# Full-height edge products with zero padding in a fused attention and MLP kernel

## The chip, the cores and the metric

One core of one Trainium2 chip runs the program. The metric is the device time of one execution in microseconds (us); the kernel before was timed three times.

## The reference

Eight batches, eight heads of 64 elements, 512 local and 32 global tokens per batch. A local query sees the local keys within 32 places of it and all 32 global keys; a global query sees every key. Each has its own softmax. The attention output of all 4352 tokens then goes through an MLP with a GELU and weights of 512 x 2048 and 2048 x 512.

```python
k_all = np.concatenate([k_g, k_l], axis=2)
out_g = np.matmul(sm(scale * np.matmul(q_g, k_all.transpose(0, 1, 3, 2))), np.concatenate([v_g, v_l], axis=2))
s_ll = np.where(np.abs(pos[:, None] - pos[None, :]) <= 32, scale * np.matmul(q_l, k_l.transpose(0, 1, 3, 2)), -1e9)
a_l = sm(np.concatenate([scale * np.matmul(q_l, k_g.transpose(0, 1, 3, 2)), s_ll], axis=-1))
out_l = np.matmul(a_l, np.concatenate([v_g, v_l], axis=2))
x = np.concatenate([out_g, out_l], axis=2).transpose(0, 2, 1, 3).reshape(B * S, H * D)
return gelu(x @ w_in) @ w_out
```

## The kernel before

**Numbers.** All products run in float32r. An operand is split into a rounded part (hi) and the rest (lo), and two or three partial products are summed.

**Units and chunks.** The attention of the local queries goes in 64 units, each of one batch, one half (256) of its 512 local queries and one pair of heads. The MLP goes in 17 chunks of 256 tokens, 16 of them a half batch each, the last the global queries of all batches. While TensorE works on the MLP of one half batch, the units of the next are made beside it. The MLP's products are `ml_h` (L865 to L867, three products of 256 columns for each of 4 row blocks) and `ml_o` (L889 to L891, 512 columns); its intermediate goes through ScalarE's GELU (`gf`), a rounding copy (`gh`, L379 to L381) and GpSimd's subtraction (`gl`, L386).

**A unit** loads its keys and queries, transposes them, and makes scores (`st_s`, L605: twelve products of 64 rows, the two heads of the pair on rows 0 to 63 and 64 to 127). Mask, exponential and scaling follow. `st_t` (L688 to L691) transposes the weights on TensorE, `st_ah` and `st_al` (L702) copy and split them into `at`, and `st_o` (L719) multiplies them with the values `vs`. `st_c` and `st_x` bring the output `o` into `xs`, which the MLP reads.

**The edge product of a unit.** A unit has two tiles of 128 queries. One tile sits next to an end of the sequence and sees 64 keys besides its own 128 (32 global ones, 32 neighbours): `st_o` of each head has three products over 128 rows and a fourth over these 64 edge keys. The values of the 64 edge keys lie in one slot of `vs`, head 0 in partitions 0 to 63 and head 1 in 64 to 127; the matching weights lie the same way in `at0[:, :, 3]`. The fourth product so reads 64 rows, `er = slice(64 * j, 64 * j + 64)` (L713, L717).

**Values.** `load_v` (L505) brings a unit's values into `vr` (7 slots of 64 elements), `split_v` (L527) makes `vs`: a copy for the hi part (L529; by ScalarE for the units of the first batch, by VectorE later) and a subtraction on GpSimd for the lo part (L530). The buffers of `vr`, two of them, are shared with the values of the global queries and with the output tile `ob`.

**Global queries.** `gu_o` (L823) makes five products for a pair of heads: four over 128 keys, the fifth over the 32 that remain, `a[:k, n]` with k = 32.

**Order.** Every step has a place in a list (`at`, L921), set by a table of offsets; the list sets the order of TensorE's instructions exactly (L1059), and of the table functions on ScalarE. The order of the other instructions on VectorE, ScalarE, GpSimd and the DMA queue of SyncE is worked out by a scheduler that takes each when it finds it ready.

Of the kernel before, what the change touches and what calls it, by code (L numbers as in the profile page):

```python
# [8 lines left out]
F32 = mybir.dt.float32  # L9
F32R = mybir.dt.float32r  # L10
# [7 lines left out]
# Products run in float32r. An operand x is split exactly into hi = round(x)  # L18
# and lo = x - hi, which float32r both holds without loss, and the partial
# products of the parts are summed in float32.  # L20
#
# Attention goes by units (batch, half of its local queries, pair of heads),
# the MLP by chunks of 256 tokens (a half batch; the global queries of all
# batches make the last chunk).  Units of one half batch are worked out while
# the MLP of the half batch before is on the tensor engine.
#
# A unit has two tiles of 128 queries: "simple" (next to an end of the
# sequence) and "full".  Blocks of 32 keys, G = the global keys:
#   half 0: keys [0 1 2 3 G 4 5 6 7 8]
#       simple window [0 1 2 3 G 4]        edge rows (G, 4)  # L30
#       full window   [3 G 4 5 6 7 8]      edge rows (3, G, 8, -)
#   half 1: keys [7 8 9 10 11 G 12 13 14 15]
#       simple window [11 G 12 13 14 15]   edge rows (11, G)
#       full window   [7 8 9 10 11 G 12]   edge rows (-, 7, G, 12)
NB = 10            # key blocks of a unit
WS, WF = 192, 224  # window widths
# [3 lines left out]
# Places of the steps in the order of the program, relative to their plain  # L40
# places, and (E_) the engines of steps that several engines can do.
# [282 lines left out]
def attn_mlp(ctx, tc, q_l, k_l, v_l, q_g, k_g, v_g, w_in, w_out, out):  # L324
    nc = tc.nc
# [4 lines left out]
    P = 128  # L330
# [23 lines left out]
    for half in range(2):  # L354
        m = cp.tile([P, WS + WF], BF16, name=f"mask{half}")
        nc.gpsimd.memset(m, 0.0)
        # (column, first key block's distance in keys from the tile's first
        # query, width) of the local key runs of the windows
        if half == 0:
            runs = [(0, 0, 128), (160, 128, 32),  # L360
                    (WS, -32, 32), (WS + 64, 0, 160)]
        else:
            runs = [(0, -32, 32), (64, 0, 128),
                    (WS, -32, 160), (WS + 192, 128, 32)]
        for c0, k0, w in runs:
            v = m[:, c0:c0 + w]
            # keep where q - k + 32 >= 0 and k - q + 32 >= 0
            nc.gpsimd.affine_select(out=v, in_=v, pattern=[[-1, w]], base=32 - k0,
                                    channel_multiplier=1, compare_op=ALU.is_ge, fill=-BIG)
            nc.gpsimd.affine_select(out=v, in_=v, pattern=[[1, w]], base=32 + k0,  # L370
                                    channel_multiplier=-1, compare_op=ALU.is_ge, fill=-BIG)
        masks.append(m)
# [30 lines left out]
    # They come as float64; word 1 of an element has sign, exponent and the  # L403
    # first 20 bits of the fraction.  As a float32 pattern times 2^-112 its
    # exponent has float32's offset, and three bits further to the left it is
    # the float32 pattern, lacking three bits of word 0 and the sign.
    # Blocks of 512 elements are kept as hi | lo.
# [49 lines left out]
    vs = cp.tile([P, 7, 2, D], F32R, name="vs")  # L457
# [4 lines left out]
    sgr = [cp.tile([P, R], F32, name=f"sgr{j}") for j in range(2)]  # L462
    gs = cp.tile([P, NP, P], F32R, name="gs")
# [3 lines left out]
    def late_tiles():  # L467
        # in the place of the weights' raw words
        wx.close()
        lp = ctx.enter_context(tc.tile_pool(name="lp", bufs=1))  # L470
        late["xg"] = lp.tile([P, NP, CH], F32, name="xg")
        late["vgs"] = lp.tile([P, 10, 2, D], F32R, name="vgs")
        late["agt"] = lp.tile([P, 5, 2, 2, SG], F32R, name="agt")

    # Blocks of 32 tokens x 32 elements of a pair of heads, for the transposes
    # of blocks: partitions are (head, half of the elements, token).
# [25 lines left out]
    # Values: slots are (tile 0, head 0), (tile 0, head 1), (tile 1, ...), the  # L502
    # full tile's edge rows for head 0 and 1, the simple tile's edge rows with
    # head 0 in the lower and head 1 in the upper partitions.
    def load_v(u):  # L505
        b, half, p = u
        raw = ap_.tile([P, 7, D], F32, name="vr", tag="vr", bufs=2)
# [15 lines left out]
        for r0, src, s0 in es:  # L523
            for j in range(2):
                nc.sync.dma_start(out=raw[64 * j + r0:64 * j + r0 + 32, 6, :], in_=src[j, s0:s0 + 32, :])
# [6 lines left out]
    def st_v(u):  # L532
        split_v((u,), vs, 7)

    # Exponentials and gelus stay in the order in which they are written here:
    # each change between them is a load of ScalarE's tables.
# [38 lines left out]
    def st_tg(b):  # L575
        # columns of a pair's scores for the globals: (hi, lo), head, query
# [8 lines left out]
    def windows(half):  # L585
        # (first key column, width, query tile) of the simple and the full tile
        if half == 0:
            return (0, WS, 0), (96, WF, 1)
        return (128, WS, 1), (0, WF, 0)

    # both heads at once (j = 0): the heads of a pair are on different rows of the tensor engine
# [17 lines left out]
    # columns of the simple and the full tile's windows; 224:256 stays zero  # L609
# [5 lines left out]
    def own(half):  # L615
        # columns of the tiles' own keys
        return (256, 64) if half == 0 else (96, 288)
# [87 lines left out]
    def st_o(u, j):  # L705
# [7 lines left out]
        er = slice(64 * j, 64 * j + 64)  # L713
# [3 lines left out]
              (vs[er, 6], at0[er, :, 3, :], qs)]  # L717
# [4 lines left out]
    # o holds [V hi; V lo] x [A hi | A lo]  # L722
# [60 lines left out]
    def gu_t(g, i):  # L783
        # transposes of one pair's rows: [key, (head, query)]
# [31 lines left out]
    # o: rows (head, A hi or lo, query), columns (head, V hi or lo, element)  # L816
    def gu_o(g, i):
        a = late["agt"]
        o = ps_s.tile([P, 2, 2, D], F32, name="go", tag="s")
        st[g, "o"] = o  # L820
        for n in range(5):
            k = P if n < 4 else 32
            nc.tensor.matmul(out=o, lhsT=a[:k, n].rearrange("p h l q -> p (h l q)"),  # L823
                             rhs=late["vgs"][:k, 2 * n:2 * n + 2], start=(n == 0), stop=(n == 4))
# [116 lines left out]
    for n, u in enumerate(units):  # L941
# [3 lines left out]
        # places between the MLP's products  # L945
# [148 lines left out]
```

## Time and profile before

| | |
|---|---|
| time, median of 3 runs | 1170.29 us (1169.29 to 1170.46) |
| span of the profiled execution | 1168.5 us, first to last instruction; no separate time of that execution is on record |
| PE (TensorE) busy | 1072.6 us, 92% |
| DVE (VectorE), ACT (ScalarE), POOL (GpSimd) busy | 775.4, 648.8, 444.2 us |
| granted TensorE clock, mean | 0.992 |

The rows of the profile name an engine, a line of the kernel, the operation, what is written and read (`o<-at,vs`), its rows and columns in the array (`64*128`), and the size of what streams through. PEld is the load of a product's stationary operand, which runs beside the products. A row of the timeline begins with the start in us from the span's start and the duration; equal neighbours are merged, with their count behind an x. Products overlap in it: each is drawn with a latency of some 0.28 us while the next starts 0.12 us after it, so distances between starts, not durations, tell what a product costs the engine.

### The profile page before, as it was taken

The page shows a single profiled execution, that of the slowest core. Times are in us where ns is not written, and L with a number is a line of the kernel's source. Part 1 is how long each engine was busy: PE and PEld are TensorE (multiplying, and loading weights), DVE is VectorE, ACT ScalarE, POOL GpSimd, SP SyncE. Part 2 cuts the span into 40 slices and gives each one's busy share as a digit, 9 for nine tenths or more (in the row PEclk, how much of TensorE's full clock was granted, in tenths as well). Part 3 has the DMA queues.
Part 4 walks back from the last instruction along what each step waited for, and adds up shares of the span by engine and source line. Part 5 has one row for each costly group of instructions (what it writes and reads, how often), then busy time and mean ns, then how long its engine had stood idle before and what let it go on. Part 6 is the DMA issues. An engine that isn't in the chain of part 4 may idle for free.

```text
span 1168.5 us, 21956 instructions
## 1 busy us (share of the span) xinstructions
PE 1072.6 (92%) x7104; PEld 931.0 (80%) x7104; DVE 775.4 (66%) x2281; ACT 648.8 (56%) x1566; POOL 444.2 (38%) x418
## 2 busy tenths in 40 slices
PE   0354789999999999999999999999999999999998
PEld 0234678888888888888888888888888888888996
DVE  7999997677756676567756776667656776653000
ACT  2454567456555665566656665566556655664222
POOL 5434545333433344334333433333433433343221
PEclk9999889999999999999999999999999999999999
DMA  7355423213221232123221322133212322121000
GB/s 210 99 139 137 114 72 77 41 27 77 55 64 26 64 66 57 33 55 67 63 45 41 63 53 64 21 77 61 55 30 64 65 54 41 42 49 32 1 19 19
DMA packets 283123, 71.21 MB, mean 61 GB/s; under 512 B 268417, under 2 KB 276609, under 8 KB 283009
## 3 DMA queue, kind: packets, MB, share of 16 engines
q1 hardware_dynamic: 272256, 53.04, 22.0%
q10 hardware_dynamic: 10752, 16.78, 4.7%
q8 instruction: 56, 0.92, 0.3%
q14 instruction: 59, 0.48, 0.1%
HBM read 60.82 MB, written 8.91 MB: 60 GB/s over the span
## 4 chain that ended last, share of the span: by engine, by line
PE 77%; DVE 10%; DMA 3%; issue 3%; ACT 3%; SPq 2%; POOL 1%; ACTq 0%; DVEq 0%; POOLq 0%
PE h L865 11%; PE acc L889 10%; PE h L867 10%; PE h L866 10%; PE acc L891 9%; PE acc L890 9%; PE o L719 7%; PE s L605 3%; PE go L823 2%; PE t L688 2%; DMA wraw<-in_moe_w_in_dram 2%; DVE wraw L434 1%; DVE a_t L624 1%; PE sg L747 1%; DVE wraw L433 1%
## 5 line engine op out<-in xcount | busy, mean ns | idle before, releaser
L386 POOL TENSOR_TENSOR gl<-gf,gh 128x512 fp32r<-128x512 f32 x136 | 180.5, 1327 | 360.7 <-ACT gh L379 197.3
L865 PE MATMUL h<-xh,wi 128*128 128x256 f32 x1088 | 316.6, 291 | 0.0
L866 PE MATMUL h<-xl,wi 128*128 128x256 f32 x1088 | 305.8, 281 | 0.0
L867 PE MATMUL h<-xh,wi 128*128 128x256 f32 x1088 | 305.5, 281 | 0.0
L889 PE MATMUL acc<-wo,gh 128*128 128x512 f32 x544 | 225.7, 415 | 0.4 <-DVE gh L381 0.4
L865 PEld LDWEIGHTS h<-xh,wi 128*128 128x128 f32 x1088 | 205.7, 189 | 15.3 <-issue 0.6
L891 PE MATMUL acc<-wo,gh 128*128 128x512 f32 x544 | 214.8, 395 | 0.0
L890 PE MATMUL acc<-wo,gl 128*128 128x512 f32 x544 | 212.8, 391 | 0.8 <-POOL gl L386 0.8
L866 PEld LDWEIGHTS h<-xl,wi 128*128 128x128 f32 x1088 | 206.2, 190 | 6.0
L867 PEld LDWEIGHTS h<-xh,wi 128*128 128x128 f32 x1088 | 205.9, 189 | 0.0
L540 ACT ACTIVATE gf<-h 128x512 f32<-128x512 f32 x136 | 81.4, 598 | 165.4 <-PE h L867 156.2
L530 POOL TENSOR_TENSOR vs<-vr,vs 128x448 fp32r<-128x448 f32 x64 | 75.5, 1179 | 236.2 <-DVE vs L381 133.3
L540 ACT ACTIVATE a_t<-a_t,sm 128x192 f32<-128x192 f32 (+1 forms) x256 | 116.9, 458 | 56.3 <-DVE sm L630 55.9
L540 ACT ACT_TABLE_LOAD x91 | 116.8, 1283 | 47.3 <-PE h L867 45.8
L702 DVE TENSOR_TENSOR at<-t,at 128x512 fp32r<-128x512 f32 (+1 forms) x128 | 74.8, 618 | 83.4 <-ACT at L379 83.0
L719 PE MATMUL o<-at,vs 128*128 128x256 f32 (+1 forms) x512 | 115.5, 331 | 6.9 <-DVE at L702 6.9
L891 PEld LDWEIGHTS acc<-wo,gh 128*128 128x128 f32 x544 | 102.3, 188 | 24.3
L605 PE MATMUL s<-k,q 64*128 64x192 f32 (+1 forms) x768 | 70.2, 300 | 55.2 <-ACT vs L379 27.5
L889 PEld LDWEIGHTS acc<-wo,gh 128*128 128x128 f32 x544 | 102.3, 188 | 19.5 <-DVE gh L381 0.5
L890 PEld LDWEIGHTS acc<-wo,gl 128*128 128x128 f32 x544 | 102.9, 189 | 13.5 <-POOL gl L386 1.4
L719 PEld LDWEIGHTS o<-at,vs 128*128 128x128 f32 (+1 forms) x512 | 83.0, 197 | 35.1 <-DVE at L702 7.1
L605 PEld LDWEIGHTS s<-k,q 64*128 64x128 f32 x768 | 56.2, 201 | 62.6 <-ACT vs L379 27.5
(89 smaller groups left out, 1707.1 us busy)
## 6 DMA issues: line engine op xcount, KB each, us to landing
kraw<-in_k_l_dram SPq DMA_DIRECT2D x256, 36.0 KB, 2.0
wraw<-in_moe_w_in_dram ACTq DMA_DIRECT2D x16, 512.0 KB, 4.4
wraw<-in_moe_w_out_dram ACTq DMA_DIRECT2D x16, 512.0 KB, 4.0
qraw<-in_q_l_dram SPq DMA_DIRECT2D x256, 32.0 KB, 1.9
vr<-in_v_l_dram SPq DMA_DIRECT2D x128, 64.0 KB, 2.1
vr<-in_v_l_dram SPq DMA_DIRECT2D x64, 128.0 KB, 2.4
out_dram<-ob SPq DMA_DIRECT2D x32, 256.0 KB, 2.1
vr<-in_v_g_dram SPq DMA_DIRECT2D x192, 16.0 KB, 1.9
```

What stands on the lines that cost most here:

```text
L386: (nc.vector if e == "v" else nc.gpsimd).tensor_sub(**kw)
L530: nc.gpsimd.tensor_sub(out=t[:, :n, 1, :], in0=raw[:, :n], in1=t.bitcast(F32)[:, :n, 0, :])
L540: x = nc.scalar.activation(func=func, **kw).ins
L605: nc.tensor.matmul(out=st[u, "s", jj][:, c:c + w], lhsT=qq[pr, qt * P:qt * P + P], rhs=kk[pr, k0:k0 + w], start=(i == 0 and n == 0), stop= ...
L702: nc.vector.tensor_sub(out=at[:, 1], in0=st.pop((u, "t", j))[:, :n * P].rearrange("p (n q) -> p n q", q=P), in1=at.bitcast(F32)[:, 0])
L719: nc.tensor.matmul(out=o[:, :, qsl], lhsT=l.rearrange("p s e -> p (s e)"), rhs=r, start=(n == 0), stop=(n == 3), skip_group_check=True)
L865: nc.tensor.matmul(out=h, lhsT=hi, rhs=xh[:, c], start=(c == 0), stop=False, skip_group_check=True)
L866: nc.tensor.matmul(out=h, lhsT=hi, rhs=xl[:, c], start=False, stop=False, skip_group_check=True)
L867: nc.tensor.matmul(out=h, lhsT=lo, rhs=xh[:, c], start=False, stop=(c == NCC - 1), skip_group_check=True)
L889: nc.tensor.matmul(out=acc[t], lhsT=gh[:, f % 2, tsl], rhs=hi, start=(f == 0), stop=False)
L890: nc.tensor.matmul(out=acc[t], lhsT=gl[:, f % 2, tsl], rhs=hi, start=False, stop=False)
L891: nc.tensor.matmul(out=acc[t], lhsT=gh[:, f % 2, tsl], rhs=lo, start=False, stop=(f == NF - 1))
```

## The change

The fourth product of `st_o` and the fifth of `gu_o` now read all 128 rows; the rows that do not belong to them are multiplied by zeros.

- `vs` and `vr` get an eighth slot. The edge values of head 0 go to slot 6, partitions 0 to 63, those of head 1 to slot 7, partitions 64 to 127. `st_v` sets the other half of both slots to zero with two GpSimd memsets (64 partitions x 64 elements) before `split_v`, whose copy and subtraction now cover 8 slots. The same DMAs load the same bytes.
- `st_o` takes slot 6 + j and all of `at0[:, :, 3]`.
- The fifth block of the global weights, `agt[:, 4]`, is set to zero once in `late_tiles`, by one VectorE copy from a part of a score tile that stays zero; `gu_o` reads 128 rows of it.
- Comments are taken out of the file; blank lines stand in their place. Line numbers of the changed kernel lie a few lines higher: the subtraction of `split_v` is L535, the memsets are L539 and L540, `st_o`'s product is L726.

```diff
-    vs = cp.tile([P, 7, 2, D], F32R, name="vs")
+    vs = cp.tile([P, 8, 2, D], F32R, name="vs")
...
+    zero = a_ts[1][:, 0, 224:256].unsqueeze(1).unsqueeze(1).to_broadcast([P, 2, 2, 32])
...
         late["agt"] = lp.tile([P, 5, 2, 2, SG], F32R, name="agt")
+        nc.vector.tensor_copy(out=late["agt"][:, 4], in_=zero)
...
-        raw = ap_.tile([P, 7, D], F32, name="vr", tag="vr", bufs=2)
+        raw = ap_.tile([P, 8, D], F32, name="vr", tag="vr", bufs=2)
...
-                nc.sync.dma_start(out=raw[64 * j + r0:64 * j + r0 + 32, 6, :], in_=src[j, s0:s0 + 32, :])
+                nc.sync.dma_start(out=raw[64 * j + r0:64 * j + r0 + 32, 6 + j, :], in_=src[j, s0:s0 + 32, :])
...
-        split_v((u,), vs, 7)
+        raw = st[u, "vr"]
+        nc.gpsimd.memset(raw[64:128, 6, :], 0.0)
+        nc.gpsimd.memset(raw[0:64, 7, :], 0.0)
+        split_v((u,), vs, 8)
...
-        er = slice(64 * j, 64 * j + 64)
...
-              (vs[er, 6], at0[er, :, 3, :], qs)]
+              (vs[:, 6 + j], at0[:, :, 3, :], qs)]
...
-            k = P if n < 4 else 32
-            nc.tensor.matmul(out=o, lhsT=a[:k, n].rearrange("p h l q -> p (h l q)"),
-                             rhs=late["vgs"][:k, 2 * n:2 * n + 2], start=(n == 0), stop=(n == 4))
+            nc.tensor.matmul(out=o, lhsT=a[:, n].rearrange("p h l q -> p (h l q)"),
+                             rhs=late["vgs"][:, 2 * n:2 * n + 2], start=(n == 0), stop=(n == 4))
```

The order of TensorE's instructions is the same in both kernels. On GpSimd, in the middle of the program (a place that comes once in each batch), the order before is, where `ge` is the scaled edge weights, `gl` the MLP's lo part and `vs` the values' subtraction:

```order
L670 TENSOR_TENSOR ge<-a_t_147,sm 128x256
L676 TENSOR_TENSOR ge<-a_t_147,sm 128x128
L386 TENSOR_TENSOR gl<-gf,gh 128x512
L530 TENSOR_TENSOR vs<-vr,vs 128x7x64
L386 TENSOR_TENSOR gl<-gf,gh 128x512
L530 TENSOR_TENSOR vs<-vr,vs 128x7x64
```

and in the changed kernel:

```order
L678 TENSOR_TENSOR ge<-a_t_147,sm 128x256
L684 TENSOR_TENSOR ge<-a_t_147,sm 128x128
L539 MEMSET vr 64x64
L540 MEMSET vr 64x64
L539 MEMSET vr 64x64
L540 MEMSET vr 64x64
L386 TENSOR_TENSOR gl<-gf,gh 128x512
L535 TENSOR_TENSOR vs<-vr,vs 128x8x64
L539 MEMSET vr 64x64
L540 MEMSET vr 64x64
L386 TENSOR_TENSOR gl<-gf,gh 128x512
L535 TENSOR_TENSOR vs<-vr,vs 128x8x64
```

The memsets of a unit stand ahead of an MLP subtraction `gl` that comes before the unit's own subtraction; here both units' memsets do, and these two buffers held the output tile `ob` before, so the memsets wait for the output's DMA.

On VectorE the order is the same after about the first 175 us (but for the copy in `late_tiles`); it differs before, while the weights are being made (`wraw`, `wi`, `wo`). Around the second unit's scores, where `sgr` frees a score buffer for TensorE, it was:

```order
L381 CAST wo<-wraw 128x512
L381 CAST q_143<-qt 128x256
L645 TENSOR_SCALAR sm<-sm 128x4
L381 CAST wi<-wraw 128x512
L386 TENSOR_TENSOR q_144<-qt,q_143 128x256
L646 RECIPROCAL sm<-sm 128x4
L759 TENSOR_TENSOR sgr_150<-sg,sgt 64x288
L676 TENSOR_TENSOR ge<-a_t_146,sm 128x128
```

and in the changed kernel:

```order
L443 SCALAR_TENSOR_TENSOR wraw<-wraw 128x512
L381 CAST q_143<-qt 128x256
L653 TENSOR_SCALAR sm<-sm 128x4
L766 TENSOR_TENSOR sgr_150<-sg,sgt 64x288
L386 TENSOR_TENSOR q_144<-qt,q_143 128x256
L654 RECIPROCAL sm<-sm 128x4
L381 CAST wo<-wraw 128x512
L684 TENSOR_TENSOR ge<-a_t_146,sm 128x128
L563 STREAM_TRANSPOSE kt<-kraw 128x128
L563 STREAM_TRANSPOSE kt<-kraw 128x160
L564 STREAM_TRANSPOSE kt<-kgr 128x32
L766 TENSOR_TENSOR sgr_150<-sg,sgt 64x288
```

The second `sgr` stands behind one more weight copy, `ge` and three transposes, and the weight copies ahead of it come earlier.

## The prediction

> **What bounds the kernel now.** First the busy time by stage, with the cuts set where TensorE's idle time ends (175 us) and where VectorE's work ends (1075 us).
>
> ```profile
> core 0: us, PE busy (x) PEld busy (x) DVE busy (x) ACT busy (x) POOL busy (x), PEclk, DMA share, GB/s
> 100.00:175.00 75.00, 54.21 (x319) 46.54 (x319) 71.67 (x164) 41.51 (x94) 36.33 (x28) 0.89 0.41 106
> 175.00:1075.00 900.00, 896.65 (x6104) 781.82 (x6104) 609.97 (x1893) 541.39 (x1319) 340.80 (x318) 1.00 0.25 52
> ```
>
> Until 175 us VectorE is the busy engine (71.67 of the last 75 us there): it makes the weights. From 175 to 1075 us TensorE is busy for 896.65 of 900 us at a granted clock of 1.00, VectorE for two thirds. The waits of TensorE after 180 us are almost nothing:
>
> ```profile
> PE gt L790 <- DVE sm L624: 1.7, 7, 0.4
> PE go L823 <- DVE agt L802: 1.1, 2, 0.7
> ```
>
> So a shorter row of products shows in the time, as long as nobody else is late. "Busy" does not say what the products cost; that is read from the distance of their starts. The timeline of TensorE at one `st_o` inside the MLP:
>
> ```profile
> 611.73 0.82 PE L719 MATMUL o<-at,vs 128*128 128x256 f32 x4
> 612.48 0.38 PE L865 MATMUL h<-xh,wi 128*128 128x256 f32 x1
> 612.70 0.28 PE L866 MATMUL h<-xl,wi 128*128 128x256 f32 x1
> 612.82 0.28 PE L867 MATMUL h<-xh,wi 128*128 128x256 f32 x1
> ```
>
> Two full products of 256 columns in a row start 0.118 us apart (here 0.12, 612.70 to 612.82). From 611.73 to 612.82 six such products start, four of `o` and two of `h`: 0.71 us would do, and it is 1.09. The 0.38 us too many lie around the 64-row product, the fourth: its own start comes late, the next product's start (612.48) comes late, and the one after that again (0.22 behind it). Single starts from the trace, rows not merged, give 0.387 us here. The MLP's products pass from 256 to 512 columns and back without such a loss; what is different here is only the number of rows.
>
> The fifth product of `gu_o`, with 32 rows, is the test of that reading:
>
> ```profile
> 581.08 0.94 PE L823 MATMUL go<-vgs,agt 128*128 128x256 f32 x5
> 581.95 0.93 PE L719 MATMUL o<-at,vs 128*128 128x256 f32 x4
> 582.81 0.39 PE L865 MATMUL h<-xh,wi 128*128 128x256 f32 x1
> 583.03 0.28 PE L866 MATMUL h<-xl,wi 128*128 128x256 f32 x1
> 583.15 0.28 PE L867 MATMUL h<-xh,wi 128*128 128x256 f32 x1
> ```
>
> Eleven products start between 581.08 and 583.15, 2.07 us instead of 11 x 0.118 = 1.30: 0.77 us for two edge products, 0.385 each.
>
> **The gain, worked out.** The counts after 176 us:
>
> ```profile
> L719 PE MATMUL o<-at,vs 64*128 64x256 f32 x115 | 43.8, 381 | 0.0
> L823 PE MATMUL go<-vgs,agt 32*128 32x256 f32 x31 | 11.7, 379 | 0.0
> ```
>
> Of the 115, 26 stand right ahead of a unit's scores, which have 64 rows themselves. The first, the last and one in the middle of these 26:
>
> ```profile
> 187.08 1.04 PE L605 MATMUL s<-k,q 64*128 64x192 f32 x12
> ...
> 614.00 0.83 PE L719 MATMUL o<-at,vs 128*128 128x256 f32 x4
> 614.45 1.04 PE L605 MATMUL s<-k,q 64*128 64x192 f32 x12
> ...
> 615.75 0.39 PE L890 MATMUL acc<-wo,gl 128*128 128x512 f32 x1
> ...
> 1020.39 1.04 PE L605 MATMUL s<-k,q 64*128 64x192 f32 x12
> ```
>
> and one of `st_s` without an edge product ahead:
>
> ```profile
> 597.20 0.28 PE L867 MATMUL h<-xh,wi 128*128 128x256 f32 x1
> 597.41 0.93 PE L605 MATMUL s<-k,q 64*128 64x192 f32 x12
> ...
> 598.61 0.39 PE L890 MATMUL acc<-wo,gl 128*128 128x512 f32 x1
> ```
>
> With the edge product small, the change of height comes before it and 614.00 to 615.75 takes 1.75 us. Made full, three steps of 0.118 lead to the edge product, and from a full product over the scores to L890 it is 598.61 - 597.20 = 1.41: 1.76 in all. These 26 gain nothing: the change of height only moves to the scores. The other 89 + 31 = 120 have full products on both sides and lose both changes: 120 x 0.386 = 46.3 us. The edge product itself stays, at the 0.118 of its neighbours.
>
> **The rule that speaks against it.** The Trainium skill, "TensorE: Matmul & The Clock Gate", Part 3 on packing small matmuls, says that products on different row groups run at the same time and that a single product of 32 rows takes as long as one of 128, so that filling rows up gives concurrency away for nothing. The trace agrees on the concurrency (the scores at 614.45 start beside the edge product), and differs on the single product, which costs 0.386 us more among full ones. By that rule alone the change would bring no gain, and its price is a rival below.
>
> **What is added, and where it hides.** GpSimd gets 128 memsets. The trace has no memset of 64 x 64; these are the nearest:
>
> ```profile
> L461 POOL MEMSET a_t<- 128x960 f32 x2 | 1.8, 894 | 0.0
> L1078 POOL MEMSET const-float32-1.0<- 128x1 f32 x1 | 0.1, 98 | 0.0
> L530 POOL TENSOR_TENSOR vs<-vr,vs 128x448 fp32r<-128x448 f32 x64 | 75.5, 1179 | 236.2 <-DVE vs L381 133.3
> L530 POOL TENSOR_TENSOR vgs<-vr,vgs 128x640 fp32r<-128x640 f32 x32 | 50.4, 1575 | 28.7 <-DVE vgs L381 19.0 <-DVE sm L645 5.3 <-DMA vr<-in_v_g_dram 1.6
> ```
>
> Between 0.10 us for one element and 0.89 for 960, I take 0.15 for 64, 0.3 per unit. The subtraction of 8 slots instead of 7 grows by 64 x (1575 - 1179) / 192 = 132 ns. So GpSimd gets about 0.43 us per unit, 57 units after 175 us: 25 us on an engine that works 341 of 900. The unit's own subtraction waited 133 us in all for VectorE's copy, so the memsets fall into waiting time there; the one who could suffer is `gl`, which now stands behind memsets. At the place shown in the order, the memsets wait for the output's DMA, second issue 579.90, which landed 2.0 to 2.9 us after its issue:
>
> ```profile
> 582.38 1.28 POOL L386 TENSOR_TENSOR gl<-gf,gh 128x512 fp32r<-128x512 f32 x1 [2.20 <-ACT gh L379]
> 586.03 0.39 PE L890 MATMUL acc<-wo,gl 128*128 128x512 f32 x1
> L904 SPq DMA_DIRECT2D out_dram<-ob x2: 368/368/368, 577.5 to 579.9; - x2
> DMA to landing us min/median/max: 2.0/2.5/2.9
> ```
>
> GpSimd is idle from 580.18 (2.20 before) to 582.38. With the landing at 582.8 and two memsets after it, `gl` begins at 583.1 and ends at 584.4; TensorE asks for it at 586.03. Cover 1.6 us, cost nothing; without it, 0.7 us at each of some 16 such places, 11 us.
>
> VectorE's copy of `vs` grows from 7 to 8 slots and ScalarE's likewise, a tenth of a microsecond at most; one zero copy in `late_tiles`: nothing I could measure.
>
> **What is late next.** TensorE comes about 0.8 us per unit earlier to products that others feed. The chunk's first product is the tightest place whose work ahead has edge products in it:
>
> ```profile
> 560.83 1.68 PE L719 MATMUL o<-at,vs 128*128 128x256 f32 x8
> 561.90 0.54 DVE L555 STREAM_TRANSPOSE kt<-kraw 128x128 f32<-128x128 f32 x2
> 565.25 0.75 DVE L386 TENSOR_TENSOR xl<-xs,xh 128x256 fp32r<-128x256 f32 x2
> 566.40 0.28 PE L865 MATMUL h<-xh,wi 128*128 128x256 f32 x1
> ```
>
> The two `st_o` at 560.83 hold two edge products, 0.77 us. VectorE works without a pause from 561.90 to the `xl` that ends at 566.00, so it will not come earlier by all of it; the slack is 0.40. Up to 0.37 us is lost, 15 chunks: 0 to 5.6 us. I take 3.5, for smaller waits too.
>
> **Before 175 us** TensorE waits anyway. Nine isolated edge products there are worth at most 9 x 0.386 = 3.5 us; VectorE's other order moves scores by a few weight copies (a score buffer is freed later behind copies of 0.3 to 0.7 us) without adding work. I take 0, and 4 us either way.
>
> **Sum.** Span 1168.5 - 46.3 + 3.5 = 1125.7; the runs' median lies 1.8 us over the profiled span, so 1127.5 us. What a measurement can tell from no change is about 0.2%, 2.3 us.
>
> **Rivals.**
> - *Other engines eat a good part* (chance 0.14). If GpSimd's 25 us came onto TensorE's path through `gl`, together with the 5.6 us of the chunk starts, 1170.3 - 46.3 + 25 + 5.6 = 1154.6. Against it speaks GpSimd's idle time of 559 us in the 900; for it, that `gl` begins right as its input comes, so that any GpSimd delay there is passed on. Half of that, about 1140, is likelier than the whole.
> - *The loss stays where it is, and the change makes the kernel slower* (0.03). If the 0.386 us belongs to the place (last product of a group, its signal to ScalarE) and not to the number of rows, full rows change nothing at the 120 places, and at the 26 the scores no longer start beside the edge product: 26 x 0.118 = 3.1 us, 1173.4. It decides as soon as a padded product still delays the one behind it by 0.2 us. Against it: `acc` and `h` groups end in the same way without a loss, and the scores (64 rows) show a late start too, 597.20 to 597.41.
> - *The first 175 us change* (0.08): VectorE's order costs or saves some 8 us; 1119 or 1136.
>
> **How the numbers follow.** My forecast has 0.75. The range goes from 1120 (all gains, those before 175 us too, nothing eaten: 1170.3 - 46.3 - 3.5 = 1120.5) to 1143, just over the half-eaten case; the fully eaten one and the slower one stay out. Faster by over 0.2%: 0.95; within: 0.02; slower: 0.03.
>
> **What would show it.** In the profile after, `st_o` amid the MLP takes 0.47 us from its first start to the next product, rows 128*128 throughout; scores still begin 0.21 after the product ahead. Stage 175 to 1075 shrinks by over 40 us with TensorE's waits at a few us. GpSimd's busy time is near 470 us. I am wrong if starts behind a padded product are still late, or if waits of `acc` for `gl`, or of `h` for `xl`, add up to over 10 us.

## The result, and the profile after

| | before | after |
|---|---|---|
| median of 4 runs | 1170.13 us (1169.29 to 1170.46) | 1141.02 us (1140.85 to 1142.11) |
| span of the profiled execution | 1168.5 us | 1140.3 us (its time 1142.11) |

The ratio is 0.975, with a 95% interval of 0.9736 to 0.9764. The change saves 29.1 us. 42.8 us were forecast, so the time lies in the range and 13.5 us above the forecast itself.

First a place like the one that the prediction measured, TensorE's timeline of the changed kernel at two `st_o` amid the MLP (start, duration, engine, line):

```profile
550.82 1.12 PE L726 MATMUL o<-at,vs 128*128 128x256 f32 x8
551.77 0.28 PE L871 MATMUL h<-xh,wi 128*128 128x256 f32 x1
551.89 0.28 PE L872 MATMUL h<-xl,wi 128*128 128x256 f32 x1
```

The `h` behind the eight products of `o` starts 0.95 us after the first of them, 0.119 for each, and the next one 0.12 later. Before, the same eight took 1.61 us, from 560.83 to the start of `h` at 562.44, and the next one came 0.23 later. The place where scores follow:

```profile
601.38 0.65 PE L726 MATMUL o<-at,vs 128*128 128x256 f32 x4
601.96 0.93 PE L613 MATMUL s<-k,q 64*128 64x192 f32 x12
602.82 0.50 PE L895 MATMUL acc<-wo,gh 128*128 128x512 f32 x1
603.15 0.40 PE L896 MATMUL acc<-wo,gl 128*128 128x512 f32 x1
```

From the first `o` to L896 it is 1.77 us; before it was 1.75. The loss has moved from the edge product to the scores, as forecast, and nothing is gained there.

Now where the rest went. The stages of the changed kernel, cut at the same places:

```profile
core 0: us, PE busy (x) PEld busy (x) DVE busy (x) ACT busy (x) POOL busy (x), PEclk, DMA share, GB/s
100.00:175.00 75.00, 51.57 (x307) 45.69 (x307) 70.42 (x156) 41.92 (x95) 37.71 (x32) 0.89 0.42 106
175.00:1075.00 900.00, 888.70 (x6298) 795.41 (x6297) 616.86 (x1912) 548.36 (x1336) 370.86 (x436) 1.00 0.25 53
```

In the 900 us TensorE starts 6298 products instead of 6104, and it now has 11 us of idle time where it had 3. In the 75 us ahead it gets through 12 products fewer. Its waits from 175 us on, the longest groups (total, times, longest):

```profile
PE go L829 <- DVE agt L809: 7.5, 11, 1.2
PE h L872 <- DVE xl L386: 1.2, 1, 1.2
PE gt L797 <- DVE sm L632: 0.8, 1, 0.8
PE t L696 <- DVE xs L741: 0.8, 1, 0.8
```

**The account.** TensorE's 7104 products come in the same order in both kernels, so the start of each can be subtracted from the start of the same one before. Product 440 is the one near 175 us.

| part of the difference, from the starts in the two traces | us |
|---|---|
| offset at product 440 | +2.8 |
| around the 120 isolated edge products (last full start ahead to the second one behind) | -45.7 |
| all other distances behind product 440 | +14.7 |
| offset of the last product | -28.2 |

The gain at the places is there in full: median 0.383 us at each, 0.33 at the smallest. 2.8 + 14.7 us were lost elsewhere. Of the 14.7, 11.6 lie in the distances ahead of 18 products that now wait over 0.05 us longer than before, 7.4 of them ahead of `go`. Another 1.1 us come from a slow clock just behind product 440, read below. The rest, some 2 us, is what many small differences of both signs leave.

**The wait of `go`.** This is one such place, TensorE:

```profile
563.55 0.28 PE L873 MATMUL h<-xh,wi 128*128 128x256 f32 x1
564.63 0.83 PE L829 MATMUL go<-vgs,agt 128*128 128x256 f32 x5 [0.80 <-DVE agt L809]
```

and the VectorE work that it waits for; the stretch, from the pause ahead of it to the `agt` that releases `go`:

```profile
547.65 1.16 DVE L710 TENSOR_TENSOR at<-t,at 128x512 fp32r<-128x512 f32 x2 [0.98 <-ACT at L379]
...
556.80 0.42 DVE L381 CAST vs<-vr 128x512 fp32r<-128x512 f32 x1
557.31 0.17 DVE L653 TENSOR_SCALAR sm<-sm 128x4 f32<-128x4 f32 x1
...
558.65 1.58 DVE L386 TENSOR_TENSOR k<-kt,k 128x320 fp32r<-128x320 f32 x1
...
563.95 0.53 DVE L809 TENSOR_TENSOR agt<-gt,agt 128x256 fp32r<-128x256 f32 x2
```

The same two places before:

```profile
557.90 1.16 DVE L702 TENSOR_TENSOR at<-t,at 128x512 fp32r<-128x512 f32 x2 [1.97 <-ACT at L379]
...
567.00 0.61 DVE L381 CAST vs<-vr 128x448 fp32r<-128x448 f32 x1
568.08 0.85 DVE L645 TENSOR_SCALAR sm<-sm 128x4 f32<-128x4 f32 x1 [0.47 <-ACT a_t L540]
...
570.11 0.45 DVE L386 TENSOR_TENSOR k<-kt,k 128x320 fp32r<-128x320 f32 x1
...
574.28 0.54 DVE L802 TENSOR_TENSOR agt<-gt,agt 128x256 fp32r<-128x256 f32 x2
```

```profile
574.82 0.28 PE L867 MATMUL h<-xh,wi 128*128 128x256 f32 x1
574.96 0.47 PE L823 MATMUL go<-vgs,agt 128*128 128x256 f32 x2
```

Before, `agt` was done at 574.82, just as TensorE came to `go` at 574.96. VectorE's stretch took 16.92 us then and takes 16.83 now, and no wait stands in it any more. TensorE's own way from the two `st_o` to `go` went from 14.13 us (560.83 to 574.96) to 12.85 without the wait: 0.77 of it for the two edge products, 0.5 elsewhere on the way. It comes about 1 us early and waits 0.96 (1.08 between the starts, less 0.12; the 0.80 in brackets counts from the modelled end of `h`). What was won at the two `st_o` is given back 13 us later.

The stretch is not VectorE's own work throughout. Its `k` lasts 1.58 us, 1.1 longer than the same step before, and lies beside this on GpSimd (before, it was `sm` at 568.08 that lasted 0.7 longer than it does now):

```profile
558.61 1.27 POOL L386 TENSOR_TENSOR gl<-gf,gh 128x512 fp32r<-128x512 f32 x1
```

At 548.73, with GpSimd idle, the same step of another unit takes 0.48 us. At all six waits of this kind (323.4, 443.9, 564.6, 685.4, 807.4 and 927.7 us, 4.2 us together) one step of VectorE, `k` or `sm`, lasts 1.1 us longer than usual beside a subtraction of GpSimd. So the length of the stretch is set by the two engines together. Nor is it unbroken at the other `go` of a batch (five waits, 3.3 us together, 1.1 of them there before): ahead of the one at 654.7 VectorE waits 0.88 us for ScalarE and 0.49 for a DMA, and its last `a_t` takes 1.88 us beside GpSimd, as it did before.

**The stage before 175 us.** TensorE's timeline there, now:

```profile
170.43 0.28 PE L873 MATMUL h<-xh,wi 128*128 128x256 f32 x1
173.61 0.73 PE L726 MATMUL o<-at,vs 128*128 128x256 f32 x4 [2.90 <-DVE at L710]
...
175.86 0.63 PE L896 MATMUL acc<-wo,gl 128*128 128x512 f32 x1
176.28 0.63 PE L897 MATMUL acc<-wo,gh 128*128 128x512 f32 x1
176.71 0.63 PE L895 MATMUL acc<-wo,gh 128*128 128x512 f32 x1
```

Before, the wait at this `o` was 0.89 us. The new one costs twice: the products behind it start 0.43 us apart instead of 0.23. The granted clock is 0.50 from 174.94 to 178.34 and 0.80 over the 7.5 us around, where it was 1.00:

```profile
170.50:178.00 7.50, 4.60 (x25) 3.48 (x25) 6.68 (x23) 2.44 (x4) 3.13 (x5) 0.80 0.29 56
174.94:178.34 3.40, 3.40 (x14) 2.62 (x11) 2.38 (x12) 0.00 (x0) 0.00 (x0) 0.50 0.18 35
```

From product 440 to product 465 this adds 1.1 us to the offset, which the table so counts in the 14.7.

**GpSimd**, the groups of the changed kernel that are new or grew:

```profile
L539 POOL MEMSET vr<- 64x64 f32 x64 | 9.6, 149 | 23.6 <-DMA out_dram<-ob 20.7 <-ACT at L379 0.3 <-ACT gos L836 0.2
L540 POOL MEMSET vr<- 64x64 f32 x64 | 9.4, 148 | 3.2
L535 POOL TENSOR_TENSOR vs<-vr,vs 128x512 fp32r<-128x512 f32 x64 | 84.2, 1316 | 222.6 <-DVE vs L381 78.7 <-DMA vr<-in_v_l_dram 41.3 <-DMA kraw<-in_k_l_dram 34.0
```

19.0 us of memsets and 8.8 us more of subtraction (64 x 137 ns) make 27.8 of the 28.2 us that its busy time grew by, to 472.4. No wait of `acc` for `gl` is in the list of waits from 175 us on, though memsets do wait for the output's DMA (20.7 us).

### The profile page after: what moved, and what is told of

Same layout as the page of the kernel before. It is cut to its first block, busy times and chain, and to the rows that moved or that the text cites. A ratio compares the mean times of both kernels' runs of the same rounds, so it can differ in the third digit from the quotient of the medians.

```text
span 1140.3 us, 22125 instructions
## 1 busy us (share of the span) xinstructions
PE 1030.7 (90%) x7104; PEld 917.9 (80%) x7104; DVE 777.6 (68%) x2282; ACT 647.6 (57%) x1566; POOL 472.4 (41%) x546
## 4 chain that ended last, share of the span: by engine, by line
PE 63%; DVE 16%; DMA 6%; ACT 5%; issue 4%; SPq 3%; POOL 1%; DVEq 0%; ACTq 0%; POOLq 0%
PE acc L895 9%; PE h L872 8%; PE h L871 8%; PE h L873 8%; PE acc L896 8%; PE acc L897 8%; PE o L726 4%; PE s L613 3%; DMA kraw<-in_k_l_dram 2%; DVE a_t L632 2%; PE t L696 2%; ACT a_t L548 2%; PE go L829 2%; DMA vr<-in_v_l_dram 2%; ACT L548 1%
## 5 line engine op out<-in xcount | busy, mean ns | idle before, releaser
L896 PE MATMUL acc<-wo,gl 128*128 128x512 f32 x544 | 214.8, 395 | 1.4 <-POOL gl L386 1.3
L535 POOL TENSOR_TENSOR vs<-vr,vs 128x512 fp32r<-128x512 f32 x64 | 84.2, 1316 | 222.6 <-DVE vs L381 78.7
L896 PEld LDWEIGHTS acc<-wo,gl 128*128 128x128 f32 x544 | 103.3, 190 | 16.6 <-POOL gl L386 4.3
L613 PE MATMUL s<-k,q 64*128 64x192 f32 (+1 forms) x768 | 67.4, 305 | 54.2 <-ACT vs L379 27.9
L613 PEld LDWEIGHTS s<-k,q 64*128 64x128 f32 x768 | 53.4, 201 | 65.6 <-ACT vs L379 27.8
L726 PE MATMUL o<-at,vs 128*128 128x256 f32 x512 | 82.0, 296 | 9.9 <-DVE at L710 9.7
L726 PEld LDWEIGHTS o<-at,vs 128*128 128x128 f32 x512 | 73.2, 201 | 13.8 <-DVE at L710 9.8
```

The costliest lines, as they stand in the source:

```text
L535: nc.gpsimd.tensor_sub(out=t[:, :n, 1, :], in0=raw[:, :n], in1=t.bitcast(F32)[:, :n, 0, :])
L613: nc.tensor.matmul(out=st[u, "s", jj][:, c:c + w], lhsT=qq[pr, qt * P:qt * P + P], rhs=kk[pr, k0:k0 + w], start=(i == 0 and n == 0), stop= ...
L726: nc.tensor.matmul(out=o[:, :, qsl], lhsT=l.rearrange("p s e -> p (s e)"), rhs=r, start=(n == 0), stop=(n == 3), skip_group_check=True)
L896: nc.tensor.matmul(out=acc[t], lhsT=gl[:, f % 2, tsl], rhs=hi, start=False, stop=False)
```

## The experiments

By the first theory, the height of the products costs 0.38 us at each isolated place and VectorE takes part of it back; by its rival, GpSimd's memsets take it back. The later kernels ask where along VectorE's work a place counts. All medians stand against runs of the kernel before of the same session (medians 1169.95 to 1170.74), and what is given back is read from one execution of each. Edits are shown against the changed kernel. "Places" is the difference around the edge products that are isolated and full, "given back" that of all other distances behind product 440, as in the account. The slow clock behind product 440 is in it, with 1.0 to 1.4 us, for the change, "only `st_o` full", "memsets twice", "28 elsewhere" and "only the 29", and not for the others.

| kernel | median us | ratio (95%) | at 440 | places | given back | wait of `go` |
|---|---|---|---|---|---|---|
| the change | 1141.02 | 0.975 (0.9736 to 0.9764) | +2.8 | -45.7 (120) | 14.7 | 7.5 |
| only `gu_o` full | 1159.57 | 0.9904 (0.989 to 0.9919) | +0.6 | -11.6 (31) | 0.1 | 0.4 |
| only `st_o` full | 1151.68 | 0.9831 (0.9815 to 0.9848) | +2.3 | -34.1 (89) | 13.0 | 5.8 |
| additions alone | 1173.0 | 1.0018 (1.0009 to 1.0027) | +1.8 | 0 | 0.4 | 0.9 |
| memsets twice | 1143.67 | 0.9769 (0.9755 to 0.9784) | +3.9 | -45.7 (120) | 16.2 | 8.5 |
| batch 0 as before | 1138.25 | 0.9724 (0.9706 to 0.9743) | +0.7 | -44.9 (118) | 12.3 | 7.0 |
| 29 in the stretch left at 64 rows | 1143.79 | 0.9781 (0.9767 to 0.9796) | +3.0 | -34.5 (91) | 7.4 | 2.2 |
| 28 elsewhere left at 64 rows | 1148.59 | 0.9818 (0.9803 to 0.9833) | +3.4 | -35.0 (92) | 10.6 | 6.9 |
| only the 29 in the stretch full | 1167.63 | 0.9982 (0.9973 to 0.9991) | +2.8 | -11.2 (29) | 6.0 | 4.3 |

### Only the global product

The kernel before, with the part of the change that concerns `gu_o`:

```diff
+    zero = a_ts[1][:, 0, 224:256].unsqueeze(1).unsqueeze(1).to_broadcast([P, 2, 2, 32])
...
+        nc.vector.tensor_copy(out=late["agt"][:, 4], in_=zero)
...
-            k = P if n < 4 else 32
-            nc.tensor.matmul(out=o, lhsT=a[:k, n].rearrange("p h l q -> p (h l q)"),
-                             rhs=late["vgs"][:k, 2 * n:2 * n + 2], start=(n == 0), stop=(n == 4))
+            nc.tensor.matmul(out=o, lhsT=a[:, n].rearrange("p h l q -> p (h l q)"),
+                             rhs=late["vgs"][:, 2 * n:2 * n + 2], start=(n == 0), stop=(n == 4))
```

> Only the global queries' fifth product over 128 rows (with its one zero copy); the local edge products stay at 64 rows, no memsets, 7 slots. 31 isolated changes of height go, at 0.38 us each by the trace after: 11.8 us. Theory A (each removed change of height shortens TensorE's row by 0.38 us; what the full change gave back, 14.7 us of waits of TensorE after about 175 us and 2.8 us before, comes from VectorE's long unbroken stretches ahead of the first go of each half batch, which start before the two local edge products): no edge product of st_o gets shorter here, so no stretch is overtaken: 1170.1 - 11.8 = 1158.3, plus or minus 1.5; waits of go for agt stay near 1.1 us. Theory B (what was given back comes from GpSimd's memsets and longer subtraction): the same 1158.3, since there are none. Theory C (the changes of height cost nothing, the place does): 1170.

1159.57 us, 11.0 saved. 31 places give 11.6 us and 0.1 is given back. The wait of `go` stays small, since the products made cheaper are behind `go`'s start and not ahead of it:

```profile
PE gt L792 <- DVE sm L626: 2.0, 7, 0.6
PE go L824 <- DVE agt L804: 0.4, 1, 0.4
```

This is the plain part of the change: no GpSimd work, and a row height alone is worth 0.37 us at each place.

### Only the local product

```diff
-        nc.vector.tensor_copy(out=late["agt"][:, 4], in_=zero)
...
-            nc.tensor.matmul(out=o, lhsT=a[:, n].rearrange("p h l q -> p (h l q)"),
-                             rhs=late["vgs"][:, 2 * n:2 * n + 2], start=(n == 0), stop=(n == 4))
+            k = P if n < 4 else 32
+            nc.tensor.matmul(out=o, lhsT=a[:k, n].rearrange("p h l q -> p (h l q)"),
+                             rhs=late["vgs"][:k, 2 * n:2 * n + 2], start=(n == 0), stop=(n == 4))
```

> Only the local edge products over 128 rows, with memsets and 8 slots; the global fifth product stays at 32 rows. 89 isolated changes of height go: 89 x 0.383 = 34.1 us. Theory A: 14.7 us of waits and 2.8 us before 175 us are given back as in the full change, since both come with the local products: 1170.1 - 34.1 + 17.5 = 1153.5, plus or minus 2; waits of go for agt about 7.5 us by the profile. Theory B: the same time, by the memsets, but with the waits at acc for gl.

1151.68 us. Most of the loss is in this half of the change: 13.0 of the 14.7 us, and 2.3 of the 2.8 at product 440.

### The additions alone

Eighth slot, memsets, larger copies and the zero copy stay; the products go back to 64 and 32 rows, out of the new slots.

```diff
-              (vs[:, 6 + j], at0[:, :, 3, :], qs)]
+              (vs[64 * j:64 * j + 64, 6 + j], at0[64 * j:64 * j + 64, :, 3, :], qs)]
...
+            k = P if n < 4 else 32
...
```

> All that the change adds (8 slots, two memsets per unit, the longer copy and subtraction, the zero copy, and the same order of instructions on all engines as in the changed kernel), but the products read 64 and 32 rows as before, from the new slots. No change of height goes. Theory A: the additions hide in the steady part; only the 2.8 us of the first 175 us remain, from VectorE's other order: 1173, plus or minus 1.5. Theory B: the 17.5 us that were given back are theirs and show here in full: 1187. Something between, 1178 say, would split the loss.

1173.0 us, 0.18% slower. The order on every engine is that of the changed kernel. Behind product 440 all the additions together cost 0.4 us; the rest is the 1.8 us ahead of it. So the additions hide as long as TensorE is the slow one. Of the 2.8 us at product 440, 1.8 come with the additions and the order, without any product of full height. TensorE comes to the `o` near 175 us 1.2 us later than in the changed kernel, waits 0.81 us there instead of 2.90, and no slow clock follows.

### The memsets twice

```diff
-        nc.gpsimd.memset(raw[64:128, 6, :], 0.0)
-        nc.gpsimd.memset(raw[0:64, 7, :], 0.0)
+        for _ in range(2):
+            nc.gpsimd.memset(raw[64:128, 6, :], 0.0)
+            nc.gpsimd.memset(raw[0:64, 7, :], 0.0)
```

> The changed kernel with each memset issued twice, four per unit. VectorE, ScalarE and TensorE keep the order of the changed kernel. Theory A: GpSimd has room, 1141.0 plus or minus 1.5. Theory B: GpSimd's additions (two memsets and the longer subtraction, about 0.43 us per unit) cost 17.5 us; two more memsets, 0.3 us, add some 10 us: 1150.

GpSimd's busy time grows by 19 us, to 491.3; the kernel takes 1143.67 us, 2.7 more. That is 1.2 over the margin written down, and far from the rival's 1150. GpSimd isn't free, then, but what it takes is a seventh of what is put on it; 1.1 us of it lie ahead of product 440. The memsets fall as the explanation of 14.7 us. GpSimd's subtractions were not varied alone, and beside them VectorE's steps last longer, as shown above.

### `go` later in the order

```diff
-    'go00': -4.0197,
+    'go00': 0.9803,
...
-    'go10': -0.7737,
+    'go10': 0.7263,
```

> The changed kernel with the first go of each half batch moved back in TensorE's order by an offset in the table (12 products later in one half batch, 17 in the other, 1.4 us and 1.7 us of TensorE's work, before the second go). Theory A: VectorE's stretch ends where it did, but TensorE has other work till then: the 7.5 us of waits of go for agt mostly go, 1141.0 - 7 = 1134, plus or minus 2. Theory A2 (VectorE's lag hits whatever comes next, so that the wait only moves to the next product that needs VectorE): 1139 to 1141, with the waits under other names.

1150.83 us (ratio 0.9823, 0.9803 to 0.9842), 16.8 over what was expected. The wait of `go` is gone, and this has come, on the same VectorE, a few steps further on:

```profile
PE gx L842 <- DVE gos L837: 14.5, 14, 1.2
```

`go`'s result goes through `gos` to `gx`, whose place was left where it was, right behind the new place of `go`. The kernel shows only that a chain was made too short; on the theory it says nothing.

### VectorE with more work

```diff
-        nc.vector.transpose(out=t, in_=st.pop((u, "raw"))[0].rearrange("p c e -> p (c e)"))
+        raw = st.pop((u, "raw"))[0].rearrange("p c e -> p (c e)")
+        for _ in range(2):
+            nc.vector.transpose(out=t, in_=raw)
```

> The changed kernel with the transposition of a unit's queries done twice on VectorE (128x256, about 0.38 us more per unit; two lie in each stretch ahead of the first go). Theory A: each stretch grows by 0.76 us, and with 15 of them TensorE waits about 11 us more: 1152, plus or minus 3; waits of go for agt near 18 us. Theory D (the stretch is set by ScalarE's exponentials and table loads, VectorE only follows): at most 3 us more, 1144.

1153.35 us (ratio 0.9848, 0.9833 to 0.9864): the total is as expected, the split is not. 4.8 us of the 12.3 come before product 440, and the 7.5 after it do not stand at `go`:

```profile
PE go L831 <- DVE agt L811: 4.5, 5, 1.7
PE gt L799 <- DVE sm L634: 4.4, 9, 0.8
PE o L728 <- DVE at L712: 2.5, 1, 2.5
```

VectorE's order changed with the edit, so this is no clean doubling, and the 12.3 us can't be put down to VectorE's work alone. The kernel decides nothing.

### VectorE with less work

```diff
-    'E_k21': 'v',
+    'E_k21': 'p',
```

> The changed kernel with the keys' second part (a subtraction of 128x320, 0.4 us on VectorE, one per unit after the first batch) on GpSimd. Theory A: each stretch loses two of them, 0.8 us, about what TensorE gained there; waits of go for agt fall to about 1 us and the time to 1134, plus or minus 2, unless GpSimd's gl comes late by then (56 x 0.9 us more on it). Theory D: 1141 or more.

1158.27 us (ratio 0.9895, 0.988 to 0.991), a miss by 24. The step went to GpSimd, and the waits are all over the place:

```profile
PE go L829 <- DVE agt L809: 5.2, 7, 1.2
PE sg L754 <- DVE xg L853: 2.7, 6, 0.5
PE h L871 <- DVE xh L381: 2.3, 4, 0.9
PE acc L896 <- POOL gl L386: 2.2, 6, 0.4
```

The relief that the kernel was to test was paid for on another engine, so this one decides nothing about VectorE either. `acc` waits for `gl` here, as it never does in the changed kernel.

### The first batch as before

```diff
-                nc.sync.dma_start(out=raw[64 * j + r0:64 * j + r0 + 32, 6 + j, :], in_=src[j, s0:s0 + 32, :])
+                nc.sync.dma_start(out=raw[64 * j + r0:64 * j + r0 + 32, 6 + j if b else 6, :], in_=src[j, s0:s0 + 32, :])
...
+        if u[0] == 0:
+            split_v((u,), vs, 7)
+            return
...
-              (vs[:, 6 + j], at0[:, :, 3, :], qs)]
+              (vs[:, 6 + j], at0[:, :, 3, :], qs) if u[0] else
+              (vs[64 * j:64 * j + 64, 6], at0[64 * j:64 * j + 64, :, 3, :], qs)]
```

> The changed kernel, but the 8 units of the first batch keep the form of before (7 slots, 64-row edge products, no memsets), with which VectorE's and ScalarE's order until 175 us is that of before. Theory A: the offset of 2 to 3 us that TensorE has at 175 us comes from that order: 1141.0 - 2.5 = 1138.5, plus or minus 1; four of the first batch's edge products run amid the MLP, so up to 1.5 us may be lost again. If the offset comes from elsewhere: 1141 or up to 1142.5.

1138.25 us, within 0.3 of what was expected. VectorE's order while the weights are made is that of before again, the offset at product 440 falls from 2.8 to 0.7 us, the wait of 2.90 us is 0.42, and no slow clock follows it:

```profile
171.67 0.93 PE L730 MATMUL o<-at,vs 128*128 128x256 f32 x4 [0.42 <-DVE at L713]
```

So most of the loss around 175 us comes from what the change does to batch 0: slot, memsets, order and products together. The additions and the order alone make 1.8 of it, as shown above; how the rest comes about is not shown. This kernel has the lowest median of all; its interval (0.9706 to 0.9743) just overlaps that of the change.

### Which edge products are worth nothing

If VectorE's stretch of 17 us sets the time at `go`, then a cheap edge product that TensorE does during that stretch buys nothing, and one outside it buys its 0.38 us. The `st_o` of the odd pairs of half 1 stand inside. Two kernels leave a number of products at 64 rows, one inside:

```diff
-              (vs[:, 6 + j], at0[:, :, 3, :], qs)]
+              (vs[:, 6 + j], at0[:, :, 3, :], qs) if u[1] == 0 or u[2] % 2 == 0 else
+              (vs[64 * j:64 * j + 64, 6 + j], at0[64 * j:64 * j + 64, :, 3, :], qs)]
```

> The changed kernel, but the units of the second half and the odd pairs (whose two edge products TensorE does while VectorE is in the stretch ahead of a batch's two first go) keep 64-row edge products; memsets, slots and the order on all engines are those of the changed kernel. 29 isolated changes of height after 175 us come back: 11.1 us. Theory A: TensorE no longer overtakes VectorE there, so about 8.5 us of its waits go at the same time: 1141.0 + 11.1 - 8.5 = 1143.6, plus or minus 2, waits of go for agt near 1 us. Theory E (the waits come from the whole program's faster pace or from what was added, not from these places): 1141.0 + 11.1 = 1152.

and one elsewhere (half 0's odd pairs):

```diff
-              (vs[:, 6 + j], at0[:, :, 3, :], qs)]
+              (vs[:, 6 + j], at0[:, :, 3, :], qs) if u[1] == 1 or u[2] % 2 == 0 else
+              (vs[64 * j:64 * j + 64, 6 + j], at0[64 * j:64 * j + 64, :, 3, :], qs)]
```

> The control to the run before: as many edge products (28 isolated ones) go back to 64 rows, those of the odd pairs of the first half, which do not lie in those stretches. Theory A: 10.7 us come back and the waits stay: 1151.7, plus or minus 1.5, waits of go for agt near 7 us. Theory E: the same 1152, so that only the difference between these two runs tells: 8 us in A, 0 in E.

The 29 isolated products inside gave 11.2 us at their places, the 28 elsewhere 10.7; the kernel lost 2.8 us when the ones were left at 64 rows, 7.6 with the others. If the place didn't matter, both losses would be alike. The medians are 4.8 us apart. The two profiled executions are 3.2 apart, and 1.0 of that is the slow clock behind product 440, which the second has and the first hasn't; how many of the other executions have it is not known. What the place decides without doubt is the wait of `go`. Left at 64 rows inside, the list of waits begins:

```profile
PE go L830 <- DVE agt L810: 2.2, 4, 0.9
```

and left at 64 rows elsewhere:

```profile
PE go L830 <- DVE agt L810: 6.9, 11, 1.1
```

In the first kernel all six waits of the kind read above are gone, and the 2.2 us stand at the other `go` of a batch; in the second kernel all six stay. At the place read above, the first kernel has `go` again right behind VectorE, without a wait:

```profile
552.40 1.68 PE L727 MATMUL o<-at,vs 128*128 128x256 f32 x8
...
566.16 0.28 PE L874 MATMUL h<-xh,wi 128*128 128x256 f32 x1
566.31 0.83 PE L830 MATMUL go<-vgs,agt 128*128 128x256 f32 x5
```

13.91 us from `o` to `go`, with the two edge products at their old price; with them full it was 13.81. They buy 0.10 us of their 0.77 here.

### Only those in the stretch

```diff
-              (vs[:, 6 + j], at0[:, :, 3, :], qs)]
+              (vs[:, 6 + j], at0[:, :, 3, :], qs) if u[1] == 1 and u[2] % 2 == 1 else
+              (vs[64 * j:64 * j + 64, 6 + j], at0[64 * j:64 * j + 64, :, 3, :], qs)]
...
+            k = P if n < 4 else 32
...
```

> Only the edge products of the second half's odd pairs read 128 rows; all other edge products, the global fifth ones too, read 32 or 64; additions and order as in the changed kernel. 29 changes of height go, 11.1 us. Theory A: TensorE gets to go earlier and waits there, some 8.5 us; with the additions alone at 1173.0: 1173.0 - 11.1 + 8.5 = 1170.4, plus or minus 2, as if nothing had been gained. Theory E: 1162.

1167.63 us, between the two: against the additions alone the 29 products, 11.2 us at their places, buy 5.4, or 4.7 when each is taken against the kernel before of its own session. The theory had them buy 2.6, which was too harsh: of 11.2 us some 6 are given back, 1.4 of them by the slow clock. The waits of `go` bear this out, 10 of them and shorter than in the changed kernel:

```profile
PE go L831 <- DVE agt L810: 4.3, 10, 0.9
```

### `go` and `gx` later together

Batch 0 as before, and the first `go` of the second pairs moved by the same amount as the `gx` that follows it, so that `gx` keeps its distance:

```diff
-    'go10': -0.7737,
+    'go10': 0.7263,
...
-    'gx10': -0.3424,
+    'gx10': 1.1576,
```

> The version with the first batch as before, with the first go of the second pairs moved 11 products later and the gx that follows it by as much, so that gx does not stand right behind go as it did in the run that moved go alone. Theory A: the larger of the two waits in each batch (about 0.9 us of TensorE, 7 times) goes, and gx has its 12 products in between as before: 1138.3 - 5 = 1133, plus or minus 2. If VectorE's lag only moves on: 1138.

1142.85 us (ratio 0.9774, 0.9758 to 0.979), a miss by 10 and 4.6 over the same kernel without the move. The wait is halved and others come in:

```profile
PE go L833 <- DVE agt L813: 3.7, 5, 1.5
PE go L833 <- POOL vgs L535: 3.2, 5, 0.7
PE acc L899 <- ACT ob L379: 1.5, 3, 0.7
```

The second `go` has become the first to be late, now for GpSimd's part of the values. The order is tight in several places at once; one number of the table doesn't free it. Why the move doesn't at least keep what batch 0 gave was not settled.

## Why the prediction was right, and where not

**Height of the products: right.** 120 places were forecast at 0.386 us, 46.3 in all; they gave 45.7. The 32-row half alone gave 11.6 for 31. The 26 places ahead of scores gave nothing. The rival by which the loss belongs to the place and not to the rows falls with the first fence above: a full product has no late follower. By the rule of the Trainium skill that was weighed ("TensorE: Matmul & The Clock Gate", Part 3 and the table under "Why this matters for your kernels"), the padding would have brought nothing; the runs with the global product alone and with all of it decide against that for a lone short product among full ones. Another page of the Trainium skill, "TensorEngine Tiling (Array Packing)", Key Properties, has the rule that fits: a change of the tiling mode drains TensorE. The runs agree, and set the price of going there and back at 0.38 us for these products.

**GpSimd's additions: right.** 0.15 us a memset and 132 ns more a subtraction were forecast, 0.149 and 137 measured; they hide, with 0.4 us lost behind 175 us when nothing else changes. The cover that the prediction named, 1.6 us behind `gl`, held: at the same place `gl` now ends at 573.15, 1.4 us before TensorE asks for it at 574.55.

**"What is late next": mis-sized, and named at the wrong place.** This is the step that failed. 3.5 us were taken, for the chunk's first product (`h` for `xl`) above all, where the trace after has a single wait of 1.2 us. 14.7 us were given back, 13.6 without the slow clock. About half, 7.4 us, is TensorE at `go`. For the six waits of the kind read above the bound was to be had from the trace of before: `agt` ended 0.14 us ahead of `go` at 574.96, behind 17 us in which VectorE stopped once, for 0.47 us, and that stop was for ScalarE. The prediction looked at VectorE's unbroken run up to `xl` and stopped there, 9 us short of its end. The two kernels with products left at 64 rows show that the location decides this wait (2.2 us of it against 6.9), and the one with only those in the stretch that about half of their gain is lost. The other half is 4.2 us ahead of seven products that wait longer (`xl`, `sm`, `xs` and others), 1.1 of slow clock and some 2 of small differences. It comes with the local products (13.0 against 0.1 us with the global ones), and doubled memsets add 1.5, which is little more than what two executions of one kernel differ by (1140.85 to 1142.11). Why VectorE is late, by its own work or by its steps that last longer beside GpSimd, is open; both kernels that were to give VectorE more or less work changed other things as well.

**Before 175 us: zero was taken, with 4 us either way; it is 2.8, and 3.9 with the slow clock that follows.** The prediction saw that VectorE's order changes there and held that no work is added. Order and additions alone cost 1.8 us, by the kernel that has nothing else; with the first batch as before, 0.7 is left and the slow clock is gone. A clock that falls behind a wait was no term of the sum.

**The rivals.** "Other engines eat a good part" had its half-eaten case at 1140, which is close to the result, though by another engine: it had GpSimd ahead of `acc`, and it was VectorE ahead of `go`. The upper end of the range was set by this rival, so it is partly luck that it covers the result. Two of the signs named beforehand did not come: behind product 440 the program is 31 us shorter, not over 40, and TensorE's waits add up to 10.9 us, not a few. The sign of being wrong named `acc` and `h`, and so could not see `go`. The sum with the measured terms: 1168.5 - 45.7 + 14.7 + 2.8 = 1140.3, the span.

## What to carry to other kernels

Among full products, one that uses fewer rows costs more than its length; fill it with zeros where the neighbours are full, and leave it where the neighbours are short too. Before summing a gain over many places, follow the engine that feeds TensorE from each place to the next product that needs it, and count only what its work leaves, with steps that last longer than others of their kind: here the places inside such a stretch kept a quarter to a half of their gain (2.8 of 11.2 and 5.4 of 11.2 us), those outside 7.6 of 10.7, by the medians. A step moved in an order that is tight moves the wait to its consumer, so move the whole chain or none.

## What the hardware showed beside it

- The granted clock fell to 0.50 for 3.4 us behind a single wait of 2.90 us, and products of 512 columns started 0.43 us apart, 0.23 elsewhere. Behind the wait of 0.89 at the same place before, it stayed at 1.00. Over the kernels here, waits of 2.44 to 3.52 us at this product all went with a granted clock of 0.50, for 3.4 or 6.8 us, and waits of 0.42 to 1.73 us did not. The Trainium skill, "TensorE: Matmul & The Clock Gate", Part 1, has the clock halved after an idle window of about 3.4 us; at this place a wait of 2.44 was enough.
- A step of VectorE lasted three times as long beside GpSimd's work: `k` took 1.58 us beside a subtraction of 1.27 us on GpSimd, and 0.48 with GpSimd idle. In the profile this is no wait but a longer step.
- A memset of 64 x 64 on GpSimd took 149 ns, against 98 ns for one element per partition, so two for each unit are cheap wherever the engine isn't the late one.
